# Sliding-window attention and hardswish MLP on one core: q and k of batch 1 folded in runs of 72 transposes, and the first 410 operations placed by a list

## The chip, the cores and the metric

The kernel runs on one core of one Trainium2 chip. A core has TensorE (PE, with its weight loads listed as PEld), VectorE (DVE), ScalarE (ACT), GpSimd (POOL) and SyncE (SP), which issues DMAs; POOL and ACT issue some too. The metric is the device time of one launch in microseconds (us), the median of the runs. Times on a trace count from the first instruction of the profiled execution.

## The reference

Causal attention over a window of 64 positions, for 8 batches of 8 heads, 576 positions and 64 columns; then a two-layer MLP on the 4608 tokens of 512 columns.

```python
scores = scale * np.matmul(q, k.transpose(0, 1, 3, 2))
mask = (rel >= 0) & (rel < window)            # rel = row - column, window = 64
scores = np.where(mask, scores, -1000000000.0)
attn = np.exp(scores - np.max(scores, axis=-1, keepdims=True))
attn = attn / (np.sum(attn, axis=-1, keepdims=True) + 1e-09)
x = np.matmul(attn, v)                        # heads side by side: (4608, 512)
h = x @ w_in                                  # (512, 2048)
g = h * np.clip(h + 3.0, 0.0, 6.0) / 6.0
out = g @ w_out                               # (2048, 512)
```

## The kernel before

**Tiles.** The MLP works on nine tiles of 512 tokens. For each tile, `s1_part` (line 736 holds its matmul) makes 16 chunks of h, four matmuls of 128 x 512 each, one for each pair of heads; `s1_finish` evicts a chunk by an ACT activation into `t1` (L749) and a DVE multiplication into `gT` (L754). `s2_part` (L775) then makes four blocks of 128 output rows from `gT` and `wout16`, 16 matmuls each; `s2_close` copies a block into one of five `osb` buffers (L788) and SP writes it out. These 1152 matmuls are the main work; "u" numbers the output blocks.

**Attention** of batch t + 1 is woven into tile t. q and k must stand with head columns on partitions. For batches 0 and 1 they come in by POOL's casting DMAs into `A` (L389) and are turned by PE: a fold is a set of 64 x 64 transposes against the matrix `fold`, 18 for one pair of heads (9 blocks by 2 heads). Batch 0 folds pair by pair (`fold_pair`, L513); batch 1 folds q of two pairs in one run of 36, and k of the two pairs in another (`fold_two`, L539), and each pair's result is copied from PSUM into `F` by DVE or ACT (L544, 128 x 576). From batch 2 on, SP turns whole tensors by DMA transposes (L391): Tq from nq, Tk from nk, after POOL has loaded these. `scores` (L580) fills PSUM, ACT takes the exponential into pT or p (L596), DVE multiplies by the mask (L605). A value product is `pv_rows` (L625, batches 0 and 1, followed by a normalization on DVE, L635 and L636, and a turn of the result by PE, `turn_x`, L651) or `pv` (L677, with ACT's logarithm and exponential, L683 and L686, and DVE's multiplications into xT, L697). The last 64 rows of all pairs together are the item "e".

**V.** Half of the value blocks are needed shifted by 64 rows: `shift_v` copies them within V (L456) on POOL, ACT or DVE. In batch 2, `hold` puts a one-column copy `scrap<-Tk` on POOL's queue ahead of the loads of V and of the next q and k, so POOL waits there until Tk has landed.

**Loads.** All weights come by POOL's queue: `win16` in five parts, `wout16` in four of four chunks each. POOL's order of loads is a chain (`then`), written by hand: q and k of batch 0, V, win, wout, q and k of batch 1 between the parts of wout, V of batch 1, nq and nk of batch 2.

**The order.** Every operation is first put on a list with the tiles that it reads and writes. `Plan.solve` then sets the order on each engine: again and again it takes, from all engines' candidates, the operation that could start first by its own table of costs (`act`, `dve`, `pool`, `LAT`, the landing times in `LANDED` and `NEXT`), less a rank; it chooses the PSUM tile ("n": two banks apart, "b": one tile of two banks, "a": two such) and, where there are several, the engine. The engines then run in that order, and real semaphores decide the times. `warm` matmuls on a constant tile keep PE busy until its first fold.

PSUM tiles are named pn (two), pb (one) and pa (two) in the profile.

Of the kernel before, what the change touches and what calls it, by code (L numbers as in the profile page):

```python
# [11 lines left out]
BF16 = mybir.dt.bfloat16  # L12
# [8 lines left out]

WINDOW = 64
LANDED = {
    "SP": (3000, 6210, 8070, 8430, 9600),
    "POOL": (4600, 6820, 7920, 9640, 10900, 11600, 11950, 12350, 12800, 13200),
    "ACT": (3200,),
}
NEXT = (15140, 16470, 19010, 21590, 24580, 26640, 29180, 30650, 32050, 32490, 35020, 37600, 39010, 40440, 41280, 42170, 43000, 43830, 44270, 45500, 46500, 47500, 48500, 49500, 50500, 51500, 52500, 53300, 54000)
MARGIN = 300
COLD_PE = 6500  # L30
FAR = 8.0e9


# [16 lines left out]
class Plan:  # L50
# [71 lines left out]
    def solve(self, rank, seen):  # L122
# [13 lines left out]
        for op in self.ops:  # L136
            for a in op.frees:
                holds.setdefault(a, []).append(op)
        order = []
        while left:  # L140
            best = None
            for key, lst in streams.items():
                cands = lst[:1] if key in inorder else lst[:24]
                for op in cands:
                    if any(d.start is None for d in op.deps) or any(d.start is None for d in op.follows):
                        continue
                    take, ts = [], 0.0
                    for name in op.alloc or ():
                        if name in slot_of:
                            continue  # L150
                        idle = [(t, i, s, k) for i, k in enumerate(op.kinds) for s, t in enumerate(slot_free[k])
                                if t is not None and (s, k) not in take]
                        if not idle:
# [8 lines left out]
                    for eng, (dur, emit, port) in (op.alts or {op.eng: (op.base, op.emit, op.port)}).items():  # L162
                        t = max(free.get(eng, 0.0), ts)
                        for d in op.deps:
                            lat = 0 if d.eng == op.eng and eng == "PE" else self.LAT
# [43 lines left out]
                nlane[eng] += 1  # L209
            for a in op.frees:  # L210
                holds[a].remove(op)
                until[a] = max(until.get(a, 0.0), op.done + self.LAT)
# [10 lines left out]
def kernel(  # L223
# [66 lines left out]
    def home(b, g, h):  # L290
        return 1 - h if 0 < b < ROWS_FROM and g % 2 else h
# [59 lines left out]
        return max(n / 2.4 + 2.5, 29.0)  # L351

    def act(n):
        return 160 + n / 1.2

    def dve(n, fast=1):
        return 150 + n / 0.96 / fast

    def pool(n):
        return 120 + n * 0.95  # L360
# [2 lines left out]
        return {"DVE": nc.vector.tensor_copy, "ACT": nc.scalar.copy, "POOL": nc.gpsimd.tensor_copy}[eng]  # L363

    def copy_op(n, out_ap, in_ap, engines, reads, writes, sbuf=False, prio=0, after=()):
        cost = {"DVE": dve(n) if not sbuf else 60 + n * 0.9, "ACT": act(n), "POOL": pool(n)}
        src = in_ap if callable(in_ap) else lambda: in_ap
        alts = {e: (cost[e], (lambda e=e: cpy(e)(out=out_ap, in_=src())), sbuf) for e in engines}
# [154 lines left out]
        e.frees = (name,)  # L523
        return op

    def fold_two(n, g0, b, gate, kinds=("b", "a")):

        pair = (g0, g0 + 1)
        names = tuple(("F", n, b, g) for g in pair)
        op = pe(R * 38 + 30, None, [("A", n, g) for g in pair] + ["fold"], [("ps", x) for x in names], "pick",  # L530
                alloc=names, kinds=kinds, after=gate, mode="r")

        def em():
            for j in range(R):
                for g, x in zip(pair, names):
                    to = bank(op, x).bitcast(BF16)
                    for h in range(2):
                        r, o = (slice(y * D, (y + 1) * D) for y in (h, home(b, g, h)))
                        nc.tensor.transpose(out=to[o, j * D : (j + 1) * D], in_=A[n][r, g, j, :], identity=fold[r, :])  # L539

        op.emit = em

        def ev(eng, g, x):
            cpy(eng)(out=F_[n][:, g, :].rearrange("d (p j) -> d p j", j=R),  # L544
                     in_=bank(op, x).bitcast(BF16)[:, 0:S].rearrange("d (j p) -> d p j", p=D))

        for g, x in zip(pair, names):
            alts = {e: (c, (lambda e=e, g=g, x=x: ev(e, g, x)), False) for e, c in (("DVE", dve(S)), ("ACT", act(S) - 30))}
            e = add("DVE", 0, None, reads=[("ps", x)], writes=[t_key(n, b, g)], alts=alts, stream="copy", prio=300)
            e.frees = (x,)  # L550
        return op

# [107 lines left out]
    def pv(b, x, i, after=(), stream="att", pr=300):  # L660
# [27 lines left out]
        for h, r in enumerate(rows):  # L688

            def ml(h=h, r=r):  # L690
# [4 lines left out]
                else:  # L695
# [5 lines left out]
        e.frees = (name,)  # L701
        return op


# [210 lines left out]
    for t in range(NTT):  # L915
# [28 lines left out]
        if b < B:  # L944
            if b == 1:
# [70 lines left out]
```

## Time and profile before

| | us |
|---|---|
| median of three runs | 301.04 |
| lowest, highest | 299.68, 301.72 |
| profiled execution, whole | 299.92 |
| its span, first to last instruction | 298.2 |
| PE busy in it | 287.4 |
| ACT, DVE, POOL busy | 207.6, 198.6, 121.7 |
| HBM read, written | 36.70 MB, 9.44 MB |

A busy PE is a PE with a matmul in flight, not one at its peak. The granted PE clock was 0.999 of full speed over the span. In a timeline row stand the start, the length, the engine, the line, the operation, what it wrote and read, its shape, and in square brackets how long the engine had stood idle before it and what ended that. A row with "xN" merges N instructions in a row; the length of a group reaches from the first start to the last end, and matmuls overlap, so the distance between starts is what a matmul costs. "SPq" is SP's issuing of DMAs: its length is the time in which the queue was busy issuing.

### The profile page before, as it was taken

How to read it: one execution, taken by the hardware profiler on the slowest of the kernel's cores; microseconds unless marked ns; L12 is line 12 of the kernel's file. 1: busy time of each engine (PE TensorE's matmuls, PEld its weight loads, DVE VectorE, ACT ScalarE, POOL GpSimd, SP SyncE). 2: the span in 40 equal slices, each digit the busy share in tenths (PEclk: the TensorE clock that was granted, in tenths of full speed). 3: DMA queues.
4: the chain of work that ended last, by engine and by line, in shares of the span. 5: the costliest groups of instructions: out<-in, count | busy, mean ns of one | idle time of the engine just before them, and what ended most of it. 6: DMA issues, size and time to landing. Idle time of an engine off the chain costs nothing.

```text
span 298.2 us, 6931 instructions
## 1 busy us (share of the span) xinstructions
PE 287.4 (96%) x2779; PEld 153.7 (52%) x2825; DVE 198.6 (67%) x326; ACT 207.6 (70%) x323; POOL 121.7 (41%) x171
## 2 busy tenths in 40 slices
PE   6899999999999999999999999999999999999996
PEld 6544545445544554455687554455445544444443
DVE  3778657786777975878678767878677868106700
ACT  3878665887968795778677958886787768227611
POOL 8884667059547906930991069405000000000000
PEclk9999999999999999999999999999999999999999
DMA  8999999989999999999996799969900110110011
GB/s 186 189 208 205 204 190 169 192 93 152 129 210 147 114 155 177 181 64 208 137 169 41 143 178 170 71 110 173 118 2 35 37 70 1 37 70 35 0 73 70
DMA packets 137680, 36.66 MB, mean 123 GB/s; under 512 B 126256, under 2 KB 132912, under 8 KB 137648
## 3 DMA queue, kind: packets, MB, share of 16 engines
q0 software_dynamic: 98816, 17.80, 73.9%
q1 hardware_dynamic: 38688, 18.12, 24.8%
q8 instruction: 22, 0.36, 0.5%
q10 hardware_dynamic: 144, 0.29, 0.4%
q14 instruction: 10, 0.08, 0.1%
HBM read 36.70 MB, written 9.44 MB: 155 GB/s over the span
## 4 chain that ended last, share of the span: by engine, by line
PE 82%; DMA 11%; POOL 4%; issue 2%; ACT 0%; POOLq 0%
PE pn L775 36%; PE pn L736 16%; PE pa L736 12%; PE pb L736 9%; DMA Ak<-in_k_dram 7%; DMA wout<-in_moe_w_out_dram 4%; PE pa L677 4%; PE pa L580 2%; PE pa L775 1%; POOL nq L389 1%; PE pb L677 1%; POOL nk L389 1%; POOL Aq L389 0%; POOL V L456 0%; PE pb L580 0%
## 5 line engine op out<-in xcount | busy, mean ns | idle before, releaser
L775 PE MATMUL pn<-wout,gT 128*128 128x512 bf16 x532 | 125.3, 379 | 2.2 <-issue 1.1
L736 PEld LDWEIGHTS <-win 128*128 128x128 bf16 x640 | 62.0, 98 | 60.5
L775 PEld LDWEIGHTS <-gT 128*128 128x128 bf16 x592 | 54.3, 98 | 57.7
L736 PE MATMUL pn<-xT,win 128*128 128x512 bf16 (+1 forms) x271 | 62.0, 357 | 0.3
L749 ACT ACTIVATE t<-pn,half 128x512 bf16<-128x512 f32 x62 | 42.7, 689 | 8.8 <-PE pn L736 8.5
L754 DVE SCALAR_TENSOR_TENSOR gT<-t,pa 128x512 bf16<-128x512 bf16 x47 | 32.2, 687 | 24.2 <-ACT t L749 23.9
L754 DVE SCALAR_TENSOR_TENSOR gT<-t,pn 128x512 bf16<-128x512 bf16 x62 | 42.6, 687 | 8.6 <-ACT t L749 8.4
L736 PE MATMUL pa<-xT,win 128*128 128x512 bf16 (+1 forms) x201 | 47.8, 358 | 0.3
L389 POOL DMA_DIRECT2D nk<-in_k_dram x55 | 41.8, 790 | 5.3 <-DMA Tk<-nk 4.6
L389 POOL DMA_DIRECT2D V<-in_v_dram x40 | 33.2, 848 | 14.4 <-PE pa L677 11.9
L749 ACT ACTIVATE t<-pa,half 128x512 bf16<-128x512 f32 x47 | 32.2, 686 | 8.9 <-PE pa L736 8.5
L697 DVE TENSOR_TENSOR xT<-pa,rec 64x512 bf16<-64x512 f32 (+1 forms) x48 | 32.0, 667 | 8.6 <-ACT rec L686 7.6
L736 PE MATMUL pb<-xT,win 128*128 128x512 bf16 (+1 forms) x153 | 36.3, 357 | 0.5 <-issue 0.5
L754 DVE SCALAR_TENSOR_TENSOR gT<-t,pb 128x512 bf16<-128x512 bf16 x35 | 24.0, 686 | 16.2 <-ACT t L749 16.1
L788 ACT COPY osb<-pn 128x512 f32<-128x512 f32 x17 | 10.0, 586 | 32.2 <-PE pn L775 32.2
L683 ACT ACTIVATE rec<-pa 64x512 f32<-64x512 f32 (+1 forms) x48 | 27.6, 574 | 4.8 <-PE pa L677 3.7
L749 ACT ACTIVATE t<-pb,half 128x512 bf16<-128x512 f32 x35 | 24.2, 690 | 7.6 <-PE pb L736 7.5
L389 POOL DMA_DIRECT2D nq<-in_q_dram x30 | 26.8, 892 | 3.3 <-DMA wout<-in_moe_w_out_dram 1.6
L596 ACT ACTIVATE pT<-pa 128x1024 bf16<-128x1024 f32 x25 | 24.6, 1021 | 1.5 <-PE pa L580 1.3
L605 DVE TENSOR_TENSOR pT<-pT,mask 128x1024 bf16<-128x1024 bf16 x28 | 18.9, 689 | 4.8 <-ACT pT L596 4.8
L677 PEld LDWEIGHTS <-V 128*128 128x128 bf16 x448 | 16.9, 98 | 6.8 <-DVE xT L697 0.5
L853 POOL COPY scrap<-Tq 128x1 bf16<-128x1 bf16 x5 | 0.9, 189 | 44.4 <-DMA Tq<-nq 44.4
(96 smaller groups left out, 205.9 us busy)
## 6 DMA issues: line engine op xcount, KB each, us to landing
out_dram<-osb SPq DMA_DIRECT2D x35, 256.0 KB, 3.6
V<-in_v_dram POOLq DMA_DIRECT2D x28, 128.0 KB, 5.9
nq<-in_q_dram POOLq DMA_DIRECT2D x24, 128.0 KB, 4.7
nk<-in_k_dram POOLq DMA_DIRECT2D x41, 64.0 KB, 4.2
wout<-in_moe_w_out_dram POOLq DMA_DIRECT2D x4, 512.0 KB, 14.5
win<-in_moe_w_in_dram POOLq DMA_DIRECT2D x3, 512.0 KB, 9.2
V<-in_v_dram POOLq DMA_DIRECT2D x12, 64.0 KB, 5.8
Aq<-in_q_dram POOLq DMA_DIRECT2D x2, 288.0 KB, 13.7
```

The lines of the kernel that those rows point to most:

```text
L389: em = lambda: e.dma_start(out=out_ap, in_=in_ap)
L580: nc.tensor.matmul(to[o, home(b, g, h) if x == "e" else h, y * D : (y + 1) * D], lhsT=w, rhs=q_cols(b, r, g, j), start=not masked, stop=no ...
L596: nc.scalar.activation(out=p_[:].rearrange("p j h c -> p h j c"), in_=wide(add_far if masked else op, name)[:, :, 0 : n * D].rearrange("p ...
L605: nc.vector.tensor_tensor(out=pp, in0=pp, in1=mask[:, m0 : m0 + n, :, :].rearrange("p j h c -> p (j h c)"), op=MULT)
L677: nc.tensor.matmul(wide(op, name)[:, h, y * D : (y + 1) * D], lhsT=V[:, blk, g, h * D : h * D + P], rhs=p_[:, y, home(b, g, h) if end else ...
L683: add("ACT", act(n), lambda h=h: nc.scalar.activation(out=rc[rows[h], 0:n], in_=wide(op, name)[rows[1 - h], h, 0:n], func=LN), reads=[key] ...
L697: nc.vector.tensor_tensor(out=o, in0=a, in1=z, op=MULT)
L736: nc.tensor.matmul(bank(op, name)[:, to : to + n], lhsT=win16[:, g, fc * P : (fc + 1) * P], rhs=xT[:, g, o : o + n], start=(g == 0), stop= ...
L749: nc.scalar.activation(out=t1[ti][:], in_=bank(op, name), func=RELU, bias=half[:], scale=1.0 / 6.0)
L754: nc.vector.scalar_tensor_tensor(out=gT[:, fc, :], in0=t1[ti][:], scalar=1.0, in1=bank(op, name), op0=MIN, op1=MULT)
L775: nc.tensor.matmul(bank(op, name)[:, 0:n], lhsT=gT[:, fc, col : col + P], rhs=wout16[:, fc, js], start=(fc == 0), stop=(fc == NFC - 1))
L788: alts = {e: (f(n), (lambda e=e: cpy(e)(out=osb[oi][:, js], in_=bank(op, name)[:, 0:n])), False) for e, f in (("DVE", dve), ("ACT", act))}
```

## The change

There are four parts.

1. `fold_two` becomes `fold_four`: one operation turns q and k of two pairs, 72 transposes in a row. q's two pairs go to the two banks of one wide PSUM tile and k's to another, and each tile is evicted by one copy of 128 x 1152 in place of two of 128 x 576. Batch 1 has two such operations where it had four.

```diff
-    def fold_two(n, g0, b, gate, kinds=("b", "a")):
+    def fold_four(g0, b, gate, kinds=("b", "a")):
...
+        names = {n: ("F", n, b, g0) for n in "qk"}
...
+            for n, x in names.items():
+                to = wide(op, x).bitcast(BF16)
+                for j in range(R):
+                    for g in (g0, g0 + 1):
+                        for h in range(2):
+                            r, o = (slice(y * D, (y + 1) * D) for y in (h, home(b, g, h)))
+                            nc.tensor.transpose(out=to[o, g - g0, j * D : (j + 1) * D], in_=A[n][r, g, j, :], identity=fold[r, :])
...
+        def ev(eng, n, x):
+            cpy(eng)(out=F_[n][:, pair, :].rearrange("d g (p j) -> d g p j", j=R),
+                     in_=wide(op, x).bitcast(BF16)[:, :, 0:S].rearrange("d g (j p) -> d g p j", p=D))
...
                 for g in range(0, NG, 2):
-                    for n in "qk":
-                        fold_two(n, g, 1, gate)
+                    fold_four(g, 1, gate)
```

2. The first 410 operations that `solve` places are taken from a list, `PLACE`, in its order; a string, `WHERE`, names the PSUM tile of each that needs one and the engine of each that has a choice. From the 411th on `solve` chooses as before.

```diff
+PLACE = (
+    0, 2, 11, 4, 12, 3, 13, 14, 24, 15, 16, 18, 41, 6, 19, 20, 21, 22, 23, 32, 33, 34, 5, 17,
...
+WHERE = "D0A1APP2A34D2D0DAD1DD4DAD301AD2D34A0123ADA4013A2413403214D02310430A2D34AA134AD0P243PDDP4P32AAA432A4AD2A3421D0432410324102341234D0AADD2341A230A4A1203"
...
-            for key, lst in streams.items():
-                cands = lst[:1] if key in inorder else lst[:24]
+            n = len(order)
+            placed = n < len(PLACE)
+            for cands in [[self.ops[PLACE[n]]]] if placed else [lst[:1] if k in inorder else lst[:24] for k, lst in streams.items()]:
```

3. The table that `solve` reckons with is changed: landing times, latencies and costs. It reaches the order from the 411th operation on, and the number of warm matmuls.

```diff
-MARGIN = 300
-COLD_PE = 6500
+MARGIN = 0
+COLD_PE = 4500
...
-    LAT = 150
+    LAT = {"PE": 150, "ACT": 150, "DVE": 70, "POOL": 70, "SP": 20}
...
     def act(n):
-        return 160 + n / 1.2
+        return 75 + n / 1.2
```

4. In `pv`, both last multiplications are noted as freeing the PSUM tile, not the second alone.

What this makes of the instructions, engine by engine: 

- PE begins with 55 warm matmuls (41 before). Its folds of batch 1 are two runs of 72, the first after eight main matmuls of tile 0's second half and the second after 28 more. The chunks of tile 0's first half come in another order (0, 3, 1, 4, 2, 6, 9, 7, 5, 12, 8, 10, 13, 15, 11, 14), and eight matmuls of the second half stand around the last chunk. The value product of batch 1's item "e" follows the first seven matmuls of tile 1. In tiles 3, 4 and 6 the second group of scores follows 8 matmuls of L775 and not 12, and value products 0 and 1, and 2 and 3, stand next to each other.
- ACT's first instructions are: a table load that the compiler puts in, the cast of k's first pair (on DVE before), two folds' evictions, the kernel's own table load (first of all before), the first exponential. It evicts four of batch 0's eight folds (six before).
- DVE builds `fold` behind the cast of q's first pair (ahead of it before). In batch 2 it does three of the four shifted copies of V (two before), the first of them ahead of the masks of pairs 2 and 3.
- SP's queue after the first loads is: out 0, Tq, out 1, out 2, out 3, Tk. Before it was: out 0, out 1, out 2, Tq, out 3, Tk.
- POOL issues the same loads in the same order, with the same operations between them, but for the shifted copies of V of batch 1: four, not five.

More of the change, by code (lines that the diff above doesn't have):

```diff
@@ L152, in solve @@
                                 if t is not None and (s, k) not in take]
+                        if placed:
+                            at = "nnbaa"[int(n := next(where))], int("01001"[int(n)])
+                            idle = [x for x in idle if x[3:1:-1] == at]
                         if not idle:
@@ L211, in solve @@
                 holds[a].remove(op)
-                until[a] = max(until.get(a, 0.0), op.done + self.LAT)
+                until[a] = max(until.get(a, 0.0), op.done + self.LAT[op.eng])
                 if not holds[a]:
@@ L365, in copy_op @@
     def copy_op(n, out_ap, in_ap, engines, reads, writes, sbuf=False, prio=0, after=()):
-        cost = {"DVE": dve(n) if not sbuf else 60 + n * 0.9, "ACT": act(n), "POOL": pool(n)}
+        cost = {"DVE": dve(n) if not sbuf else 60 + n * 0.73, "ACT": act(n), "POOL": pool(n)}
         src = in_ap if callable(in_ap) else lambda: in_ap
@@ L524, in fold_pair @@
         return op
-    def fold_two(n, g0, b, gate, kinds=("b", "a")):
[L528 to L531, printed above, removed]
-        def em():
[L534 to L539, printed above, removed]
-        op.emit = em
[L543 to L549, printed above, removed]
@@ new lines, in fold_four @@
+    def fold_four(g0, b, gate, kinds=("b", "a")):
+        pair = slice(g0, g0 + 2)
+        names = {n: ("F", n, b, g0) for n in "qk"}
+        op = pe(2 * R * 33 + 30, None, [("A", n, g) for n in "qk" for g in (g0, g0 + 1)] + ["fold"], [("ps", x) for x in names.values()],
+                "pick", alloc=tuple(names.values()), kinds=kinds, after=gate, mode="r")
+        def em():
+            for n, x in names.items():
[5 more added lines that the diff above has]
+                            nc.tensor.transpose(out=to[o, g - g0, j * D : (j + 1) * D], in_=A[n][r, g, j, :], identity=fold[r, :])
+        op.emit = em
+        def ev(eng, n, x):
+            cpy(eng)(out=F_[n][:, pair, :].rearrange("d g (p j) -> d g p j", j=R),
+                     in_=wide(op, x).bitcast(BF16)[:, :, 0:S].rearrange("d g (j p) -> d g p j", p=D))
+        for n, x in names.items():
+            alts = {e: (c, (lambda e=e, n=n, x=x: ev(e, n, x)), False) for e, c in (("DVE", dve(2 * S)), ("ACT", act(2 * S)))}
+            e = add("DVE", 0, None, reads=[("ps", x)], writes=[t_key(n, b, g) for g in (g0, g0 + 1)], alts=alts, stream="copy", prio=300)
@@ L700, in pv @@
                     writes=[("x", b % RB, g, 1 if end else 0, h) for g in gs], prio=pr + 100)
-        e.frees = (name,)
+            e.frees = (name,)
         return op
```

18 lines of the change are left out of this document (12 added, 6 removed), and 17 rows, old and new, of the table PLACE.

## The prediction

> **What bounds the kernel now.** The page first: how full TensorE (PE) is in each of 40 slices, in tenths, and what the loads and stores moved.
>
> ```profile
> PE   6899999999999999999999999999999999999996
> GB/s 186 189 208 205 204 190 169 192 93 152 129 210 147 114 155 177 181 64 208 137 169 41 143 178 170 71 110 173 118 2 35 37 70 1 37 70 35 0 73 70
> ```
>
> Only the first two of 40 slices (7.5 us each) and the last are not full, and the loads run at some 200 GB/s for the first 37 us. So a reordering can gain only where PE has holes. The chain of waits says what fills the front:
>
> ```profile
> 5.42 6.50 DMA Ak<-in_k_dram
> ...
> 14.85 11.79 DMA wout<-in_moe_w_out_dram
> ...
> 27.17 13.26 DMA Ak<-in_k_dram
> ```
>
> Up to 41 us the chain is the queue of loads, not an engine; the change keeps that order. Then PE's timeline, with its milestones:
>
> ```profile
> 5.33 0.47 PE L513 MATMUL pn<-fold,Aq 64*64 64x64 bf16 x18 [0.89 <-DVE Aq L368]
> ...
> 16.50 0.38 PE L736 MATMUL pa<-xT,win 128*128 128x512 bf16 x1
> ...
> 31.61 0.48 PE L539 MATMUL pa<-fold,Aq 64*64 64x64 bf16 x36
> 32.02 1.04 PE L775 MATMUL pn<-wout,gT 128*128 128x512 bf16 x3
> ...
> 36.04 3.63 PE L775 MATMUL pn<-wout,gT 128*128 128x512 bf16 x15
> ...
> 41.61 0.81 PE L775 MATMUL pn<-wout,gT 128*128 128x512 bf16 x3 [0.16 <-issue]
> ...
> 50.51 0.39 PE L677 MATMUL pa<-p,V 128*128 128x64 bf16 x8
> 50.74 1.03 PE L775 MATMUL pn<-wout,gT 128*128 128x512 bf16 x4
> ...
> 51.83 0.81 PE L736 MATMUL pn<-xT,win 128*128 128x512 bf16 x3
> ...
> 57.01 1.03 PE L736 MATMUL pa<-xT,win 128*128 128x512 bf16 x4
> 57.87 1.03 PE L736 MATMUL pn<-xT,win 128*128 128x512 bf16 x4
> ```
>
> A column count after a matmul's name is its shape, the number after x how often it came. Four main matmuls take 57.87 - 57.01 = 0.86, 0.216 each. Main work starts at 16.50, tile 1 at 51.83. One profiled execution has these times: span 298.2, whole 299.92, which is 1.12 below the median of three, 301.04. I take the change as a difference and add it to both.
>
> **Startup (to 37.8).** The changed program puts 55 warm matmuls for 41, the `fold` build behind the cast of Aq, the cast of Ak on ScalarE (ACT) instead of VectorE (DVE), and ACT's table load behind two copies, in front of the first exponential; a second load is put in ahead of the Ak cast, where ACT only waits for that tile.
>
> ```profile
> 1.13 3.31 PE L977 MATMUL pn<-ones 128*128 128x96 bf16 x41 [1.13 <-DVE ones L857]
> 1.24 1.28 ACT L865 ACT_TABLE_LOAD   x1 [1.24 <-PEq L1000]
> 5.84 0.64 ACT L518 COPY Fq<-pn 128x576 bf16<-128x576 bf16 x1 [3.31 <-PE pn L513]
> 7.52 1.02 ACT L596 ACTIVATE pT<-pa 128x1024 bf16<-128x1024 f32 x1
> 10.12 0.95 DVE L368 CAST V<-stage 128x512 bf16<-128x512 f32 x2 [0.61 <-DMA stage<-in_v_dram]
> 37.87 0.88 POOL L389 DMA_DIRECT2D nq<-in_q_dram  x1 [1.63 <-DMA wout<-in_moe_w_out_dram]
> ```
>
> Warm-up ends at 1.13 + 55 x 0.081 = 5.57, 0.24 later than the first fold stood. The fold takes 0.4, ACT's two copies (0.64 each) run from about 6.05 to 7.3, the load to 8.6, and the first exponential starts 1.1 after its 7.52. It ends at 9.6; the first value product also needs V, cast from 10.12 on, which has not moved. So the 1.1 is covered by that landing. From there ACT has less to do: it evicts four of the eight folds, today six, so 2 x 0.64 less stands among its four exponentials. I let a quarter of that reach main work: 16.2 (15.2 with all of it, 17.6 with all of the 1.1 lost). What it is worth is set later: the last quarter of wout lands at 37.87 by GpSimd's (POOL's) wait. PE now begins the matmuls on it at 36.04 + 8 x 0.216 = 37.77: no slack. The changed program has the same work ahead of that point, so what startup gains PE waits there. Price 0, bounds 0 to +1.1.
>
> The Trainium skill, ScalarE: Activation LUTs, section "What ACT_TABLE_LOAD costs", charges a drain of about 1.38 us beside the load's 1.28, for each switch of set. The load's row agrees; no row shows the drain, since ACT then waits anyway. By that rule startup would lose 1.4 more, a rival below; by the row alone it loses nothing.
>
> **The folds of batch 1 (37.8 to 51.83).** 144 transposes stay 144. A run of 36 takes 32.02 - 31.61 = 0.41, so 72 take 0.82. The second run needs Ak, landed at 27.17 + 13.26 = 40.43. Twelve main matmuls from 37.8 end at 40.4: it starts at 40.5 and main work resumes at 41.45, for 41.61 now: -0.16. Four wide evictions replace eight:
>
> ```profile
> L544 ACT COPY Fk<-pa 128x576 bf16<-128x576 bf16 x2 | 1.3, 639 | 0.7 <-PE pb L539 0.7
> L544 DVE COPY Fq<-pa 128x576 bf16<-128x576 bf16 x2 | 1.5, 758 | 1.6 <-PE pa L539 1.6
> ```
>
> Doubled columns cost between once and twice: ACT 0.64 to 1.28, DVE 0.76 to 1.52, side by side. Eight main matmuls (1.73) stand between each run and the scores that read it, so even 1.52 + 0.1 is hidden; with the cover gone it would be 0.9 per run. The closing value product (50.74 - 50.51 = 0.23) moves into tile 1, price 0.
>
> **The one new wait: V of batch 2 (51.8 to 83).** The load chain does not end with tile 0. SP (the DMA queue), POOL, and who waits:
>
> ```profile
> 39.45 11.41 SPq L389 DMA_DIRECT2D out_dram<-osb  x3
> 45.81 2.63 POOL L456 COPY V<-V 64x384 bf16<-64x384 bf16 x5
> 53.39 3.00 SPq L391 DMA_TRANSPOSE Tq<-nq  x1
> 56.50 0.55 SPq L389 DMA_DIRECT2D out_dram<-osb  x1
> 57.27 3.33 SPq L391 DMA_TRANSPOSE Tk<-nk  x1
> 62.44 0.19 POOL L853 COPY scrap<-Tk 128x1 bf16<-128x1 bf16 x1 [11.80 <-DMA Tk<-nk]
> 63.04 4.21 POOL L389 DMA_DIRECT2D V<-in_v_dram  x5 [0.41 <-DVE gT L754]
> 71.82 1.32 DVE L456 COPY V<-V 64x1024 bf16<-64x1024 bf16 x2
> 72.01 1.56 ACT L456 COPY V<-V 64x768 bf16<-64x768 bf16 x2
> 73.79 0.63 PE L677 MATMUL pb<-pT,V 128*128 128x64 bf16 x16
> DMA to landing us min/median/max: 3.4/4.7/5.1
> L456 DVE COPY V<-V 64x1024 bf16<-64x1024 bf16 x12 | 6.1, 510 | 0.3
> L605 DVE TENSOR_TENSOR pT<-pT,mask 128x1024 bf16<-128x1024 bf16 x28 | 18.9, 689 | 4.8 <-ACT pT L596 4.8
> ```
>
> Today: Tk starts at 57.27, has landed at 62.44 (5.17 later), V's five loads go out by 67.25, the shifted copies end at 73.57 on ACT, and PE takes them at 73.79, with 0.2 to spare. In the changed program SP has out, Tq, out, out, out, Tk: Tq stands in front of two outs that left before it. Nobody waits for those, but Tk does. POOL has four shifted copies for five (2.63 / 5 = 0.5 each) ahead of the last nq and nk issues; two of the four are the longer kind, so Tq may start up to 0.4 earlier. Tq from 53.0 to 53.4, 3.0 long; three outs at 0.55 to 0.77 (57.27 - 56.50): Tk starts at 57.7 to 58.7 and lands at 62.9 to 63.9; two more 256 KB in front of it take up to 1.25 each at the page's 205 GB/s, partly while Tk is issued: up to 1.4 more. I take 63.7, +1.3 (+0.5 to +2.9). By the Trainium skill, DMA: Bandwidth & Descriptors, section "Queues, rings and completion order", a ring's descriptors are consumed in order and SP has one row of rings, so the outs do go first; no row here isolates it.
>
> V's last load leaves at 66.4 (five issues in 4.21) and lands 3.4 to 5.1 later by the row of that stretch, at 69.8 to 71.5; I take the middle, 70.7. With +1.3 it is 72.0 (70.3 to 74.4). In the changed program DVE does one 1024 shift, then both last masks, and only then the shift of 768 columns that the first value product needs; the masks queue behind V's landing. From landing: 0.51 + 2 x 0.69 + 0.51 (the smaller shift, priced as the larger) + 0.1 = 2.5, so 74.5. PE arrives at 73.79 - 0.16 = 73.6. Stall 0.9; against 73.79 the kernel is +0.7 (-0.2 without a stall; +3.1 with both upper ends).
>
> **Later.** One `osb` copy of tile 1 moves from DVE to ACT ahead of a reciprocal's EXP:
>
> ```profile
> 76.17 0.62 ACT L686 ACTIVATE rec<-rec 128x512 f32<-128x512 f32 x1
> 76.82 1.41 DVE L697 TENSOR_TENSOR xT<-pb,rec 64x512 bf16<-64x512 f32 x2
> 78.41 0.63 PE L677 MATMUL pb<-pT,V 128*128 128x64 bf16 x16
> ```
>
> That product waits for the bank, free at 78.23, slack 0.18; a copy of about 0.5 more on ACT costs 0.3 (0 to 0.5). In tiles 3, 4 and 6 scores come four matmuls earlier and value products in pairs; PE's slices show no hole there now; with slacks like this 0.18 I estimate 0.1 each, 0.3 (0 to 1.0).
>
> Sum: 0 + 0.7 (the -0.16 is in it) + 0.3 + 0.3 = +1.3. Profiled 299.92 + 1.3 = 301.2; median 302.3.
>
> **Rivals.** *No stall (0.24)*: Tk lands by 62.8; -0.16 to +0.3, median 301.1. For it: only 0.5 more at Tk's start is certain. Against: 0.2 slack in the rows above. *Tk late (0.16), the other side*: place, SP's three outs; each us of Tk past 62.8 stalls PE one for one (70.7 - 62.44 = 8.3 to V, then 2.5), so Tk at 66.0 is 76.8, +3.0 + 0.6 = +3.6, 304.6; it is slower by over 1% from 65.4 on. For it: SP's order puts all three outs first, and Tk has the same row of rings to go through. Against: 1.4 for that queue is its upper bound. *The table load costs double (0.06)*: worked as a second 1.28 on ACT, the first exponential starts at 9.9 and ends at 10.9, past the V cast; main work starts at 17.1 for 16.5, and PE comes 0.6 late to wout's landing. V's stall of 0.9 then hides 0.6 of it: +1.3 again, up to +1.9 where V is early, 302.9. The skill's drain is this mechanism. *The loads land earlier (0.04)*: an out leaves the 40 to 45 us stretch; only a shorter load chain could give 3 us, and nothing in it is removed: 298. That the list is not followed is excluded: the instructions stand in that order.
>
> **Numbers.** 1% is 3.0 us, about what a measurement of this kernel tells from no change: 298.0 to 304.05. Forecast 0.50 (301.4 to 303.4), rivals as given. Faster 0.04; same 0.50 + 0.24 + 0.05 = 0.79; slower 0.16 + 0.01 = 0.17. Range: 300.0 (no stall, 300.9, less part of the 1.36 by which the lowest run of before, 299.68, lies under its median) to 304.4, near the late Tk.
>
> **What would show it.** Main work at 16.2 +- 0.4; PE waiting for wout near 37.8; tile 1 at about 51.4; SP's Tk start at 57.7 to 58.7 and POOL's scrap copy near 63.7; a PE hole of 0.7 before the first value product of batch 2, ended by DVE. Wrong if tile 1 starts before 50.9 (the load chain did not bind), if that hole is absent or above 2, or if a hole over 0.5 stands in a tile from 2 on.

## The result, and the profile after

| | kernel before | changed kernel |
|---|---|---|
| median of eleven runs each, us | 300.17 | 301.91 |
| lowest, highest | 299.68, 301.72 | 301.62, 302.32 |
| profiled execution, whole | 299.92 | 301.64 |
| its span | 298.2 | 299.9 |

The ratio is 1.0052, with a 95% interval of 1.0034 to 1.0071: 1.7 us slower by the medians, and 1.72 by the two profiled executions. The forecast was +1.3, which made 302.3 from the median of three, 301.04; the median of eleven for the kernel before is 0.87 lower, so the difference is the figure to compare.

On the page of the changed kernel, the chain of waits has these shares of the span.

```profile
PE 90%; DVE 4%; issue 3%; ACT 2%; DVEq 0%; ACTq 0%
```

No load is among these shares. In the kernel before, the chain ran along the queue of loads up to 41 us. Nothing of PE's work was added beyond 14 warm matmuls, so the 1.7 us must lie between PE's matmuls or in matmuls that stay in flight longer. PE's busy time does not show where: it counts a matmul in flight, and it grew from 287.4 to 289.9. So the same point of the work is looked up in both timelines of PE. First the changed kernel (start, length, what was done, how often; in brackets the idle time ahead of it):

```profile
16.42 0.59 PE L767 MATMUL pa<-xT,win 128*128 128x512 bf16 x2
...
18.07 0.38 PE L682 MATMUL pn<-ident,opg 128*128 128x128 bf16 x4 [0.63 <-issue]
...
21.16 0.29 PE L611 MATMUL pa<-Fq,Fk 64*128 64x64 bf16 x8
...
36.95 4.49 PE L806 MATMUL pn<-wout,gT 128*128 128x512 bf16 x19
...
44.63 1.90 PE L806 MATMUL pn<-wout,gT 128*128 128x512 bf16 x7
46.46 0.45 PE L656 MATMUL pa<-V,pT 128*64 128x65 bf16 x16
46.84 1.04 PE L806 MATMUL pn<-wout,gT 128*128 128x512 bf16 x4
...
51.98 1.67 PE L767 MATMUL pa<-xT,win 128*128 128x512 bf16 x7
...
57.95 1.04 PE L767 MATMUL pb<-xT,win 128*128 128x512 bf16 x4 [0.29 <-DVE xT L728]
...
66.79 0.71 PE L611 MATMUL pa<-Tq,Tk 64*64 64x64 bf16 x64
...
74.40 0.63 PE L708 MATMUL pb<-pT,V 128*128 128x64 bf16 x16
...
79.64 0.64 PE L708 MATMUL pb<-pT,V 128*128 128x64 bf16 x16 [0.46 <-DVE xT L728]
...
86.55 0.38 PE L767 MATMUL pa<-xT,win 128*128 128x512 bf16 x1
```

Then the rows of the kernel before that were not shown yet:

```profile
20.92 0.29 PE L580 MATMUL pa<-Fq,Fk 64*128 64x64 bf16 x8
...
43.04 2.76 PE L775 MATMUL pn<-wout,gT 128*128 128x512 bf16 x11
45.73 0.26 PE L625 MATMUL pa<-V,pT 128*64 128x65 bf16 x4
46.36 0.38 PE L625 MATMUL pa<-V,pT 128*64 128x65 bf16 x12 [0.37 <-POOL V L456]
...
65.74 0.71 PE L580 MATMUL pa<-Tq,Tk 64*64 64x64 bf16 x64
...
69.25 0.28 PE L580 MATMUL pa<-Tq,Tk 64*64 64x64 bf16 x10 [0.20 <-issue]
...
84.96 0.38 PE L736 MATMUL pa<-xT,win 128*128 128x512 bf16 x1
```

| point of the work | before | after | after less before |
|---|---|---|---|
| main work starts | 16.50 | 16.42 | -0.08 |
| scores of item e of batch 0 | 20.92 | 21.16 | +1.10 |
| main work behind batch 1's first scores | 36.04 | 36.95 | +0.91 |
| the same, eight matmuls ahead of value product 0 | 43.90 | 44.63 | +0.73 |
| main work behind that product | 46.67 | 46.84 | +0.17 |
| tile 1 (item e still to come in the changed kernel) | 51.83 | 51.98 | +0.15 |
| scores of batch 2 | 65.74 | 66.79 | +1.05 |
| first value product of batch 2 | 73.79 | 74.40 | +0.61 |
| third | 78.41 | 79.64 | +1.23 |
| tile 2, seventh main matmul | 84.96 | 86.55 | +1.59 |
| second half of tile 8 | 281.28 | 282.99 | +1.71 |

Two lines are corrected to equal work. At the second, the changed kernel has 16 main matmuls behind it and the other 20, so 4 x 0.216 is added to 0.24. In the fourth, 43.90 is 43.04 + 4 x 0.216. The counts in some rows are one short (x7 for eight); such a gap of one main matmul reads as "[0.16 <-issue]" and is no idle time.

So 1.1 is lost between 16.4 and 21.2, and 0.56 of it vanishes at 46, where the kernel before stood still for V (45.73 to 46.67 is 0.94 for a product of 0.38). 0.9 is lost in the first half of tile 1, 0.44 is regained in the scores of batch 2, 0.98 is lost between that batch's first value product and tile 2, and the rest, up to the second half of tile 8, adds 0.12.

### The profile page after: what moved, and what is told of

Same layout as the page of the kernel before. It is cut to its first block, busy times and chain, and to the rows that moved or that the text cites. A ratio compares the mean times of both kernels' runs of the same rounds, so it can differ in the third digit from the quotient of the medians.

```text
span 299.9 us, 6949 instructions
## 1 busy us (share of the span) xinstructions
PE 289.9 (97%) x2795; PEld 155.0 (52%) x2839; DVE 194.6 (65%) x321; ACT 209.8 (70%) x326; POOL 122.4 (41%) x170
## 4 chain that ended last, share of the span: by engine, by line
PE 90%; DVE 4%; issue 3%; ACT 2%; DVEq 0%; ACTq 0%
PE pn L806 37%; PE pn L767 17%; PE pa L767 14%; PE pb L767 10%; PE pa L708 3%; PE pa L611 3%; DVE xT L728 2%; PE pn L1007 2%; PE pa L806 1%; PE pb L708 1%; DVE V L398 1%; ACT rec L714 1%; PE pn L543 1%; PE pb L611 1%; ACT rec L717 1%
## 5 line engine op out<-in xcount | busy, mean ns | idle before, releaser
L767 PE MATMUL pn<-xT,win 128*128 128x512 bf16 (+1 forms) x262 | 60.6, 356 | 0.3
L785 DVE SCALAR_TENSOR_TENSOR gT<-t,pa 128x512 bf16<-128x512 bf16 x50 | 34.1, 686 | 30.6 <-ACT t L780 30.4
L767 PE MATMUL pa<-xT,win 128*128 128x512 bf16 (+1 forms) x215 | 50.1, 359 | 0.4
L780 ACT ACTIVATE t<-pn,half 128x512 bf16<-128x512 f32 x60 | 41.2, 688 | 8.4 <-PE pn L767 7.7
L785 DVE SCALAR_TENSOR_TENSOR gT<-t,pn 128x512 bf16<-128x512 bf16 x60 | 41.0, 686 | 7.7 <-ACT t L780 7.5
L780 ACT ACTIVATE t<-pa,half 128x512 bf16<-128x512 f32 x50 | 34.0, 686 | 11.2 <-PE pa L767 9.1
L419 POOL DMA_DIRECT2D V<-in_v_dram x40 | 33.2, 848 | 16.4 <-PE pa L708 13.8
L819 ACT COPY osb<-pn 128x512 f32<-128x512 f32 x23 | 13.4, 582 | 28.7 <-PE pn L806 28.5
L728 DVE TENSOR_TENSOR xT<-pa,rec 64x512 bf16<-64x512 f32 (+1 forms) x44 | 29.2, 664 | 5.6 <-ACT rec L717 4.7
L714 ACT ACTIVATE rec<-pa 64x512 f32<-64x512 f32 (+1 forms) x44 | 25.2, 572 | 5.5 <-PE pa L708 4.5
L627 ACT ACTIVATE pT<-pa 128x1024 bf16<-128x1024 f32 x27 | 26.6, 1021 | 2.0 <-PE pa L611 2.0
```

What stands on the lines that cost most here:

```text
L419: em = lambda: e.dma_start(out=out_ap, in_=in_ap)
L627: nc.scalar.activation(out=p_[:].rearrange("p j h c -> p h j c"), in_=wide(add_far if masked else op, name)[:, :, 0 : n * D].rearrange("p ...
L714: add("ACT", act(n), lambda h=h: nc.scalar.activation(out=rc[rows[h], 0:n], in_=wide(op, name)[rows[1 - h], h, 0:n], func=LN), reads=[key] ...
L728: nc.vector.tensor_tensor(out=o, in0=a, in1=z, op=MULT)
L767: nc.tensor.matmul(bank(op, name)[:, to : to + n], lhsT=win16[:, g, fc * P : (fc + 1) * P], rhs=xT[:, g, o : o + n], start=(g == 0), stop= ...
L780: nc.scalar.activation(out=t1[ti][:], in_=bank(op, name), func=RELU, bias=half[:], scale=1.0 / 6.0)
```

## The experiments

Each kernel lists all 1244 operations, in an order from the two kernels' own, so that an edit at one place moves nothing elsewhere. The diffs show the instruction order on an engine. All times are compared with runs of the kernel before on the same chip, which had medians of 300.31 to 300.49. The changed kernel itself was not run again beside them. Three of the edits to it gained nothing, and those runs stand at 1.0059 to 1.0061 of the kernel before, so the changed kernel's 1.0052 is if anything low. A gain is given as 1.0052 less the run's ratio.

### The two osb copies on DVE

```diff
@@ ACT, tile 1's second half @@
-TensorCopy osb_90<-pn_61 128x512
...
-TensorCopy osb_91<-pn_62 128x512
@@ DVE @@
+TensorCopy osb_90<-pn_61 128x512
...
+TensorCopy osb_91<-pn_62 128x512
```

What the edit is aimed at, in the timelines of ACT and DVE of the changed kernel:

```profile
76.90 0.59 ACT L819 COPY osb<-pn 128x512 f32<-128x512 f32 x1
77.51 0.63 ACT L717 ACTIVATE rec<-rec 128x512 f32<-128x512 f32 x1
...
78.17 1.41 DVE L728 TENSOR_TENSOR xT<-pb,rec 64x512 bf16<-64x512 f32 x2 [4.10 <-ACT rec L717]
...
83.68 1.39 DVE L728 TENSOR_TENSOR xT<-pb,rec 64x512 bf16<-64x512 f32 x2 [1.75 <-ACT rec L717]
```

DVE idles for 4.10 us until ACT has made the copy and then the reciprocal's last step; PE, at 79.64, waits for DVE.

> The changed kernel, with the second and third osb copies of tile 1 on DVE instead of ACT; the rest of the order is the same. Theory A (these two copies hold ACT ahead of the reciprocals, DVE idles 4.10 and 1.75 us for them, and PE waits for the banks): from the first value product of batch 2 (74.40) to 86.55 in tile 2 the changed kernel loses 0.98 against the kernel before; without the two copies on ACT that goes, and the time is 0.8 to 1.0 us under the changed kernel's 301.91, about 300.9 to 301.1, with the third value product near 79.0. Rival B (the order of the value products or the late V sets the loss, not the copies): no more than 0.3 us gained, 301.6 or above. The prediction's size for one such copy was 0.3.

Measured: 301.35 beside 300.48, ratio 1.0035 (1.0019 to 1.0052). In the same timelines of this run:

```profile
77.58 0.63 PE L742 MATMUL pb<-pT,V 128*128 128x64 bf16 x16
...
80.74 1.41 DVE L762 TENSOR_TENSOR xT<-pb,rec 64x512 bf16<-64x512 f32 x2 [0.24 <-ACT rec L751]
...
82.21 0.64 PE L742 MATMUL pb<-pT,V 128*128 128x64 bf16 x16
```

All of this profiled execution lies some 3 us late, for a reason told in the last section, so only distances count. From the first to the third value product it takes 82.21 - 77.58 = 4.63 (before 4.62, changed 5.24), and no hole is left. Theory A is right on the mechanism. The time fell by 0.0017, 0.5 us, less than the 0.8 forecast; the interval holds both, and taken alone it holds no gain as well. Beside two runs on the same chip that gained nothing (302.04 and 302.11, below) it is 0.7.

### Item e's exponential one place earlier

```diff
@@ ACT, tile 1 @@
 Activation rec_96<-pb_63 64x256
+Activation rec_96<-rec_96 128x256
 Activation t_0_87<-pn_62,half 128x512
-Activation rec_96<-rec_96 128x256
```

> The changed kernel, with the exponential of batch 1's item e put one place earlier on ACT, ahead of the eviction of the first pn chunk of tile 1. Theory A (item e, moved into tile 1, holds the tile pb until DVE's multiplications at 57.03 to 57.89, and PE's next pb chunk waits for it at 57.95): the multiplications come 0.6 earlier, the chunk starts at 57.5, and the time falls by 0.3 to 0.5 us to about 301.5. Rival B (what PE gains there it waits for later, at the scores of batch 2, since Tk and V set that point): no gain, 301.9, with a longer hole before a value product of batch 2.

Measured: 302.04, ratio 1.0059 (1.0046 to 1.0071): nothing gained. In this run's PE timeline the pb chunk starts without a hole, at 57.78, and the chunk behind it waits instead:

```profile
59.35 1.02 PE L801 MATMUL pa<-xT,win 128*128 128x512 bf16 x4 [0.55 <-DVE gT L819]
```

The wait was moved by one chunk: the exponential that went ahead pushed back the eviction that the next chunk needs. The rival named a later place (batch 2) for it.

### Startup in the order of the kernel before

The list up to the first fold of batch 1 is taken from the kernel before, with its 41 warm matmuls (table load first, `fold` built early, Ak cast on DVE, chunks 0 to 15 in order); the rest is the changed kernel's.

> The changed kernel, with everything up to the first run of folds of batch 1 in the order of the kernel before (41 warm matmuls, table load first, chunks 0 to 15 in order); from there on its own list. Theory A (the changed startup costs PE 0.98 us by the scores of item e of batch 0, and it is lost for good, because the changed kernel passes the last quarter of wout 0.7 to 0.9 us after it has landed and so never waits for it): PE comes to that quarter up to 0.98 earlier, of which the landing at 37.9 leaves 0.7 to 0.8; time 0.6 to 0.8 us less, about 301.2. Rival B, the prediction's price of 0 (the wait for wout swallows whatever startup gains): 301.8 to 302.0, with a hole before the matmuls on that quarter. Rival C (the V load of batch 2 sets the next point): the gain shows up to tile 1 and is gone at the first value product of batch 2.

Measured: 301.23, ratio 1.0033 (1.0020 to 1.0047), 0.6 us under the changed kernel. Its profiled execution (301.59) is slower than its median, and shows where a gain can go; the PE rows, and one of DVE:

```profile
36.04 4.54 PE L840 MATMUL pn<-wout,gT 128*128 128x512 bf16 x20
...
45.16 0.91 DVE L520 COPY V<-V 64x384 bf16<-64x384 bf16 x2 [2.75 <-DMA V<-in_v_dram]
...
46.12 0.38 PE L690 MATMUL pa<-V,pT 128*64 128x65 bf16 x12 [0.26 <-DVE V L520]
```

PE comes to 36.04 0.91 earlier than in the changed kernel, and runs through the matmuls on wout's last quarter without a hole, as the kernel before did. What then takes the gain in this execution is V of batch 1, whose landing DVE awaits for 2.75 us, and the first turn behind it (0.47 idle at 47.94). Rival B is refuted, and rival C has its mechanism right, one batch too late.

### SP's queue in the order of the kernel before

```diff
@@ SP @@
 DMACopy out_dram<-osb
+DMACopy out_dram<-osb
+DMACopy out_dram<-osb
 DmaTransposeAnt Tq<-nq
-DMACopy out_dram<-osb
-DMACopy out_dram<-osb
 DMACopy out_dram<-osb
 DmaTransposeAnt Tk<-nk
```

> The changed kernel, with outs 1 and 2 put ahead of Tq on SP's queue again, as in the kernel before. Theory A (PE reaches the first value product of batch 2 late for other reasons, so the order of SP's queue costs nothing in the changed kernel): Tk may land up to 0.9 earlier, the time stays within 0.2 us of 301.9. Rival B, the prediction's mechanism (Tk lands late, V behind it, PE waits for the shifted copies): 0.5 to 0.9 us gained, about 301.2.

Measured: 302.11, ratio 1.0061 (1.0048 to 1.0074). First the changed kernel's rows for Tk, V and the shifted copies, then this run's for the landing of Tk:

```profile
57.73 3.70 SPq L421 DMA_TRANSPOSE Tk<-nk  x1
...
63.37 0.19 POOL L884 COPY scrap<-Tk 128x1 bf16<-128x1 bf16 x1 [12.33 <-DMA Tk<-nk]
...
70.91 0.77 DVE L486 COPY V<-V 64x1024 bf16<-64x1024 bf16 x1 [0.21 <-DMA V<-in_v_dram]
...
73.02 1.05 DVE L486 COPY V<-V 64x768 bf16<-64x768 bf16 x2
```

```profile
62.17 0.19 POOL L918 COPY scrap<-Tk 128x1 bf16<-128x1 bf16 x1 [11.54 <-DMA Tk<-nk]
```

Tk lands 1.2 us earlier, and the time does not fall. (Its issue starts 0.7 earlier, at 57.04. From there it takes 5.1 to its landing, as in the kernel before, for 5.6 in the changed kernel, so the outs ahead of it cost 0.5 in the queue beside their issuing.) The order of SP's queue does what the prediction said to Tk, and Tk is not what PE waits for. Theory A holds.

### 41 warm matmuls, and 53

```diff
-                for _ in range(int((op.start - 350) * 0.95 / (IDLE / 1.2))):
+                for _ in range(41):
```

> The changed kernel with 41 warm matmuls instead of 55, nothing else. In its profile, and in two others with the same startup, PE stands still for 0.63 to 0.75 us between the first weight load and the first matmul of the fourth turn, waiting for nothing shown; that matmul is number 704 on PE, and the other such hole, of 0.7 at 12.16, stands before number 448, 256 instructions earlier. Theory A (PE's instructions come in blocks of 256 and 14 more warm matmuls, 28 instructions, bring PE to the block's end before the next block is there): with 41 the block ends 14 matmuls later; the fourth turn starts within 0.2 us of the main matmuls ahead of it, the hole is gone or moves to number 704, and the scores of item e start at 20.4 to 20.6 instead of 21.16 to 21.45. Theory B (a dependency of that turn): the hole of 0.6 to 0.8 stays ahead of the fourth turn. For the time both expect little, 301.4 to 302.0, since the value products of batch 1 wait for V and DVE next; a gain over 0.6 would show that startup sets the end.

Measured: 301.31, ratio 1.0024 (1.0012 to 1.0036). PE's timeline:

```profile
16.99 0.59 PE L801 MATMUL pa<-xT,win 128*128 128x512 bf16 x2
...
17.85 0.40 PE L716 MATMUL pn<-ident,opg 128*128 128x128 bf16 x4
...
20.96 0.29 PE L645 MATMUL pa<-Fq,Fk 64*128 64x64 bf16 x8
```

Main work starts 0.57 later than in the changed kernel's profile (in this execution PE waits 0.77 for V's last cast, at 11.77), and the fourth turn still comes 0.22 earlier: it stands right behind the main matmuls, and no hole stands before 704. The scores of item e missed the forecast 20.4 to 20.6 because of that late start; from the start of main work they take 3.97, where the changed kernel took 4.74. The time fell by 0.0028, 0.8 us, more than either theory gave: startup does reach the end.

With 53 the question is where in the turn the hole falls.

> The changed kernel with 53 warm matmuls instead of 55. Theory A (blocks of 256 instructions): the hole of 0.6 to 0.8 stays before PE's instruction 704, which is now the third matmul of the fourth turn: two of its four transposes stand ahead of the hole and two behind it; the hole of the fourth q fold moves two transposes on, to after eight of its 18. Theory B (a dependency of the turn): the hole stays ahead of all four transposes. The time within 0.4 us of the changed kernel's.

Measured, one run: 302.05. PE's timeline:

```profile
11.52 0.31 PE L577 MATMUL pn<-fold,Aq 64*64 64x64 bf16 x8
12.41 0.34 PE L577 MATMUL pn<-fold,Aq 64*64 64x64 bf16 x10 [0.59 <-issue]
...
17.67 0.28 PE L716 MATMUL pn<-ident,opg 128*128 128x128 bf16 x2
18.61 0.27 PE L716 MATMUL pn<-ident,opg 128*128 128x128 bf16 x2 [0.66 <-issue]
```

Two transposes of the turn stand ahead of the hole and two behind it, and the fold is cut after its eighth: both holes stand before instructions 448 and 704, wherever those fall. A dependency would have stayed with the turn. So Theory A is right: the holes go by the number of the instruction. What PE waits for there is read from the trace further below.

### Item e ahead of tile 1

```diff
@@ PE, start of tile 1 @@
+Matmult pa_64<-p_84,V 128x64 x8
 Matmult pa<-xT,win_66 128x512 x3
 Matmult <-xT,win_66 128x512 x4
-Matmult pb_63<-p_84,V 128x64 x8
 Matmult pa<-xT,win_66 128x512 x1
@@ ACT @@
+Activation rec_96<-pa_64 64x256 x2
+Activation rec_96<-rec_96 128x256
 Activation t_2_89<-pb_63,half 128x512
```

> The changed kernel with batch 1's item e ahead of tile 1's first matmul again, on a pa tile, its mask and its logarithms, exponential and multiplications earlier on DVE and ACT; 55 warm matmuls. Theory A (item e inside tile 1 holds up the chunk evictions: 0.45 us at 57.95 and about 0.2 more before): tile 1's first half takes 14.0 us instead of 14.8 less the product's own 0.23, and the time falls by 0.4 to 0.6, to about 301.4. Rival B (the waits only change their place, as in the run with the early exponential): 301.8 to 302.1.

Measured: 301.46, ratio 1.0029 (1.0017 to 1.0041). PE's timeline, first main matmul of tile 1 and the scores behind its first half:

```profile
52.54 0.81 PE L801 MATMUL pa<-xT,win 128*128 128x512 bf16 x3
...
66.51 0.71 PE L645 MATMUL pa<-Tq,Tk 64*64 64x64 bf16 x64
```

13.97 for the half, and no hole in it; the changed kernel takes 66.79 - 51.98 = 14.81, of which 0.23 is the product. Theory A holds: the time fell by 0.0023, 0.7 us (0.4 to 0.6 forecast).

### The folds alone

In the kernel before:

```diff
@@ PE, tile 0's second half; the same at the second pair of runs @@
-transpose pa<-fold,Aq x36
 Matmult pn<-wout,gT 128x512 x4
 Matmult pb<-p,V 128x64 x8
-transpose pa<-fold,Ak x36
+transpose pa<-fold,Aq x36
+transpose pa<-fold,Ak x36
```

> The kernel before, its own order throughout, with only the folds of batch 1 changed: two runs of 72 where the runs of k stood, wide evictions by ACT and DVE, and the last scores of batch 1 four matmuls later. Theory (the prediction's): two changes of matmul shape fewer, 0.16 us gained at most, the wide evictions hidden: 300.2 to 300.5 beside 300.4 for the kernel before. Rival (the wide evictions, 1.12 to 1.36 each, or pairs q and k that now both wait for k's load hold up the scores): 0.3 to 1.0 slower, 300.7 to 301.4.

Measured: 300.79 beside 300.43, ratio 1.0012 (0.9996 to 1.0027); no difference can be told. In its profile the stretch from behind the first scores to eight matmuls ahead of value product 0 takes 0.19 less than before (36.79 to 44.46, for 36.04 to 43.90), which is the expected size. Then PE waits 0.23 for an exponential. It is not the wide eviction that holds this up: that ends at 43.19, and ACT stands idle until the scores are there, which come four matmuls later in this order:

```profile
42.07 1.12 ACT L609 COPY Fk<-pa 128x1152 bf16<-128x1152 bf16 x1 [1.04 <-PE pa L604]
44.11 0.60 ACT L661 ACTIVATE p<-pb 128x512 bf16<-128x512 f32 x1 [0.92 <-PE pb L645]
...
46.59 0.45 PE L690 MATMUL pa<-V,pT 128*64 128x65 bf16 x16 [0.23 <-ACT pT L661]
```

### The table load first again

```diff
@@ ACT @@
+LoadActFuncSet
 TensorCopy Ak<-stage
 TensorCopy Fq<-pn x2
-LoadActFuncSet
```

> The changed kernel with the kernel's own table load first of all on ACT, as in the kernel before; 55 warm matmuls. Theory A (startup hangs on V's casts on DVE and on PE's instruction blocks, not on ACT): the first exponential starts at 7.5 to 7.6 instead of 8.87, and main work no more than 0.2 earlier; time 301.7 to 302.1. Rival B (the prediction's upper bound: the load's 1.28 in front of the first exponential reaches main work): main work 0.5 to 1.1 earlier, time 301.0 to 301.4.

Measured: 302.03, ratio 1.0061 (1.0046 to 1.0077). The compiler puts in no second load in this order, so ACT also has one load less. The first exponential starts at 8.19 (7.5 to 7.6 forecast: ACT waits for the scores), for 8.87 in the changed kernel, and main work at 16.57. Theory A holds on the time: the load in front of the first exponential costs nothing here.

### Edits together

The first takes the startup of the kernel before, the osb copies, item e and a later first turn of batch 1; the second 41 warm matmuls, the osb copies and item e; the third is the second with its warm matmuls 128 columns wide instead of 96.

> The changed kernel with its startup in the order of the kernel before, the two osb copies of tile 1 on DVE, item e ahead of tile 1, and batch 1's first turn after the second value product instead of ahead of it; the folds and everything else as changed. Theory A (these four places hold the loss, and each is kept once the others are gone): 301.9 less 0.7, 0.6, 0.5 and 0.25 is 299.8 to 300.1, a little faster than the kernel before. Rival B (the gains of startup and of item e are taken back at V of batch 2, whose transposes and loads start no earlier): about 300.6 to 301.0, with a hole ahead of the first value product of batch 2.

> The changed kernel with three edits at once: 41 warm matmuls, the two osb copies of tile 1 on DVE, item e ahead of tile 1; its startup order and everything else as changed. Theory A (the three costs are separate and add): against the kernel before the changed one stands at 1.0052, the three edits alone took 0.0028, 0.0017 and 0.0023 off that, so 0.998 to 0.999, about 0.3 to 0.6 us faster than the kernel before. Rival B (they overlap, and V of batch 2 sets the end once two are gone): 1.000 to 1.002.

```diff
-    IDLE = 96
+    IDLE = 128
```

> The run with the three edits, its 41 warm matmuls now 128 columns wide instead of 96: warm-up lasts to about 5.5 as with 55 narrow ones, with the 28 fewer instructions kept. Theory A (with 41 narrow ones PE stands still 1.29 us ahead of its first fold, and goes on slowly after it, 1.17 us for 36 transposes, so main work starts at 17.0 to 17.1 instead of 16.4 to 16.6): main work starts at 16.5 to 16.7, no hole before the fourth turn, and the time is 0.2 to 0.5 us under that run's, 0.998 to 0.999 of the kernel before. Rival B (the first folds' place does not reach main work, V's casts set it): main work again at 17.0, 0.9995 of the kernel before. Rival C (with PE earlier at the block's end the hole comes back): a hole of 0.3 to 0.7 before instruction 704.

| | us | the kernel before | ratio |
|---|---|---|---|
| startup of before, and three edits | 300.17 | 300.43 | 0.9987 (0.9974 to 1.0000) |
| three edits | 300.24 | 300.31 | 0.9995 (0.9986 to 1.0004) |
| three edits, wide warm matmuls | 300.00 | 300.49 | 0.9985 (0.9974 to 0.9996) |

The first run lies close to its theory A (299.8 to 300.1) and outside rival B. The three costs add in the main: alone they took 0.0017, 0.0028 and 0.0023 off 1.0052, 0.0068 in all; together they took 0.0057, between the two theories of that run, and each of these figures is uncertain by 0.001 or more. Counted from the 1.0060 of the runs that gained nothing, it is 0.0092 against 0.0065, so a part of them overlaps.

The last run is 0.15% faster than the kernel before, with an interval that ends just under 1. From the run with narrow warm matmuls it cannot be told apart. Its PE timeline has main work and the fourth turn where its theory put them, and a remainder of the hole before instruction 448:

```profile
12.41 0.38 PE L645 MATMUL pa<-Fq,Fk 64*128 64x64 bf16 x14 [0.36 <-issue]
...
16.65 0.59 PE L801 MATMUL pa<-xT,win 128*128 128x512 bf16 x2
...
17.52 0.40 PE L716 MATMUL pn<-ident,opg 128*128 128x128 bf16 x4
```

That the wide matmuls brought main work forward is not shown. The slow first folds, 1.17 us for 36 transposes in the run with the three edits, take 1.17 in the changed kernel too, with no idle time before them, and 0.80 in the run that has 41 narrow warm matmuls alone. There main work starts at 16.99 all the same, behind V's cast, so rival B is open.

## Why the sum was right and its terms were not

The forecast +1.3 came out as +1.7, inside the range. That it came so close is luck: the largest term, the stall at V of batch 2, did not happen, and costs that had been put at 0 stood in its place. The prediction had named its own sign: wrong if the hole before the first value product of batch 2 is absent. It is absent. The terms were:

- **Startup, price 0.** The step that failed is "Price 0": the cover named for it, PE waiting for wout's last quarter, did not bind. The changed kernel came to that quarter at 36.95 + 8 x 0.216 = 38.7, 0.7 after its landing, and lost 1.1 before it. What was foreseen held: main work at 16.42 (16.2 forecast), the first exponential late and covered (shown by the run with the table load first). What was missed is that warm matmuls were priced by their time alone; each is two instructions, too, a weight load and a matmul, and 28 more instructions brought PE to the end of a block of instructions before the next had come. Of the 1.10, the run with 41 takes out 0.77 (4.74 to 3.97); the rest was not traced. The bound +1.1 was right in size by luck: it was meant for the table load. Of the 1.1, 0.56 fell into a wait that the kernel before has at V of batch 1; its row, 46.36 with 0.37 idle, was in the timeline that the prediction quoted from, and tells that this landing, and not wout's, had no slack.
- **Folds, -0.16.** About -0.18 in the changed kernel's second run (0.91 to 0.73), -0.19 in the run with the folds alone, though no time came of it there. The size was right by luck. The prediction took it from the row at 41.61, whose "x3" is four matmuls with the first record missing; weight loads at 41.38 and 41.39 show that main work came back at 41.39 there, and 41.45 against that is no gain. The gain came from elsewhere: from its start to the next main matmul a run of 72 takes 42.33 - 0.22 - 41.37 = 0.74, where the prediction counted 0.95.
- **Item e moved into tile 1, price 0.** Wrong. Its 0.23 of PE was counted as moved; its five instructions on ACT and DVE, queued among the chunk evictions of tile 1, were not. They held a pb tile, and PE with it. The run that puts it back gains 0.7 us.
- **V of batch 2, +0.7.** The stall did not come. Tk started at 57.73 and had landed at 63.37 (57.7 to 58.7, and 63.7, forecast); V's last load went out at 67.46 and landed 3.7 later, at 71.2 and not 72.0: the prediction had taken 4.3 for this step, the middle of 3.4 to 5.1. The first copy could start at 70.91, and from there the 2.5 held: the copy that the product needs, the first of the two of 768 columns, ends at 73.44 (74.5 forecast). PE came at 74.40, late by then. The run with SP's old order shows Tk 1.2 earlier and no gain. Nor was there a hole when PE came earlier: in the run with the three edits Tk landed at 63.43, that copy ended at 73.49, and PE started the product at 73.86. So the term was wrong, and not merely hidden.
- **The osb copy, +0.3.** The mechanism was right, the count was not: two copies moved to ACT (76.90 and 81.93). The stretch from the first value product of batch 2 to tile 2 lost 0.98, and with the two copies back on DVE it takes 11.30 for 12.15, so 0.85 of it was theirs.
- **Tiles 3 to 8, +0.3.** 0.12.

A gain that the prediction had not seen made room for this: PE's hole of 0.20 at 69.25 in the kernel before. There PE loses 0.4 in the scores of batch 2 (1.06 from 68.41 to the next main matmul, 0.67 in the changed kernel). It stands before instruction 1984, which is 704 + 5 x 256, and has the same cause as the holes at 448 and 704, by the transfers below.

By the Trainium skill, Runtime: NRT & Kernel Launch, section "Instruction fetch mechanics", each engine fetches its program by its own DMA queue in blocks of 256 instructions, and the crossing is mostly hidden. The traces agree on the block, with holes before 448 and 704 in five profiles of the changed startup, and before one of them in two more, and on the queue (row below: 22 packets, 0.36 MB, for 5678 instructions of PE, 258 each). The run with the osb copies has neither hole: there PE had stood still for 2.02 just ahead of 448. Most of the 22 crossings are hidden, as the page has it, but not these: 0.20 to 0.76 each. From the page of the changed kernel:

```profile
q8 instruction: 22, 0.36, 0.4%
```

The trace has the transfers of this queue one by one, 16384 bytes each, and they show that PE waits for them. In the changed kernel one ends at 16.63 and the hole before 704 at 18.07. In the run with SP's old order they end at 10.77 and 16.87, and the holes at 12.16 and 18.36. In the kernel before one ends at 67.87, and the hole before 1984 at 69.25. All 13 holes, in eight profiles, end 1.4 to 1.5 us behind the end of a transfer.

Why the block comes late was not settled: the loads run at some 200 GB/s then, and 64 x 64 transposes with their weight loads use up a block of 256 in 1.5 us (128 by 0.41 / 36), but neither was varied.

The drain of 1.38 beside a table load that the Trainium skill states (ScalarE: Activation LUTs, section "What ACT_TABLE_LOAD costs"), weighed in the prediction as a rival, does not appear. In ACT's timeline of the changed kernel the load follows a copy that ends at 7.56, and the exponential follows the load by 0.01:

```profile
7.58 1.28 ACT L896 ACT_TABLE_LOAD   x1
8.87 1.02 ACT L627 ACTIVATE pT<-pa 128x1024 bf16<-128x1024 f32 x1
```

This is one load, behind the one that the compiler puts in at 1.25; no run shows which set that one names.

## What to carry to other kernels

A filler matmul costs instructions as well as its time: where PE idles by "issue", count its instructions up to that point, and try fewer fillers. (Wide fillers in place of narrow ones cost nothing here; that they gain is not shown, with 300.00 beside 300.24.) A piece of attention that is moved by a few matmuls takes its evictions along; look at what it holds back on ACT and DVE, not at PE's 0.23. A hole that PE already has names the landing without slack, here V's of batch 1; a wait of the loading engine, as POOL's for wout, did not.

## What the runs showed of the hardware

The granted clock fell to half while PE stood still for 2.02 us, and came back some 6 us after PE went on. In one execution of the run with the osb copies on DVE (303.97, where the other eleven took 301.02 to 301.65), V's cast came late. PE's row, then the windows (from and to, length, PE's busy us and instructions, granted clock, DMA share, GB/s):

```profile
13.03 0.64 PE L690 MATMUL pa<-V,pT 128*64 128x65 bf16 x8 [2.02 <-DVE V L432]
```

```profile
13.00:15.40 2.40, 2.37 (x62) 0.50 1.43 198
15.40:19.00 3.60, 3.60 (x60) 0.50 1.25 207
19.00:22.00 3.00, 2.97 (x34) 0.99 1.24 207
```

Holes of 0.6 to 0.8 did not do this: in the run with SP's old order the clock is 1.00 from 18.4 to 22, behind the hole of 0.75. That 2.02 is enough is read from this one execution.
